# Chunk-selected attention and a gated MLP on one core: K transposed in fp32 with its chunk bounds read from PSUM, odd heads' q and k moved by DMA, loads paced by need, weights held back until the first exps

## The chip, the cores and the metric

The kernel runs on one core of one Trainium2 chip. The metric is device time in microseconds (us) of one execution. Each kernel was executed several times; an execution is called fast or slow by its time against the fastest of the same kernel, and only fast ones are compared. The profiled span is about 2 us shorter than the device time of the same execution (296.9 for 298.89 us before).

Engine names are those of the profile: PE (TensorE matmul), PEld (TensorE weight load), DVE (VectorE), ACT (ScalarE), POOL (GpSimd), SP (SyncE, which here only issues DMAs; "SPq" is its queue). "PEclk" is the clock that TensorE was granted, as a share of full speed.

## The reference, cut to what matters

```python
# q, k, v: (4 batches, 8 heads, 768 positions, 64), fp32
k_chunks = k.reshape(B, H, 24, 32, D)
k_min, k_max = k_chunks.min(axis=3), k_chunks.max(axis=3)
ub = sum_d max(q * k_min, q * k_max)            # an upper bound per query and chunk
top_chunks = the 6 best causal chunks of every query
scores = q @ k.T / 8, masked to the chosen chunks and to the causal part
attn = softmax(scores);  x = attn @ v           # heads side by side: (4, 768, 512)
# then per batch a gated MLP:
h = gelu(x @ w_in); u, v = halves of h; v = layernorm(v) * g_ln
out = x + (u * (w_sg @ v + b_sg)) @ w_out
```

The kernel handles heads in pairs (16 pairs) and selects chunks for groups of four heads (8 groups). A batch is two groups, so there are four MLPs.

## The kernel before: the parts that the change touches

The kernel records operations with their reads, writes, engine and estimated cost. A greedy list planner in the kernel then fixes, before anything runs, the order of instructions on each engine.

Loads, weights and K's side, with cuts marked `...`:

```python
P.base = 60.0
P.op("pool", ...dma_start(winb[:], ...), 8.0, writes=["winb"], dma="winb")      # 3 weight loads,
P.op("pool", ...dma_start(woutb[:], ...), 6.0, writes=["woutb"], dma="woutb")   # ready from the
P.op("pool", ...dma_start(wsgf, ...), 8.0, writes=["wsgf"], dma="wsgf")         # first moment
P.op("sp", ...dma_start(bsgbc[:], ...), 3.0, writes=["bsgbc"], dma="bsg")
...
def loads(p):                       # one pair: k, q, v of two heads, 192 KB each
    s = p % NQS                     # NQS = 3 buffers
    for nm, src, dst in (("kn", k, kn), ("qn", q, qn), ("vn", v, vn)):
        for i in range(2):
            P.op("sp", ...dma_start(dst[s][:, :, i, :], [[DH,128],[128*DH,NT],[1,DH]]), ...)

def kside(p):
    for m, op in ((0, ALU.min), (1, ALU.max)):          # on natural K: transpose + reduce in one op
        P.op("dve", ...tensor_reduce(km[w]..., knv..., axis=AX.X, op=op, apply_transpose=True), ...)
    P.op("dve", ...tensor_tensor(km[w][:, 1], km[w][:, 1], km[w][:, 0], op=ALU.subtract), ...)
    for c in range(4):                                  # bounds to DRAM scratch ...
        P.op("sp", ...dma_start(kscr..., km[w][32*c:32*c+32]...), ...)
    P.op("sp", ...dma_start(W[w][:], kscr...), ...)     # ... and back, transposed
    P.op("pool", ...tensor_copy(kb16[p % 2], knv), ...) # K to bf16
    ...six bf16 PE transposes into one PSUM tile...
    DVE copies rows 0:64 to KA (even head), ACT copies rows 64:128 to KB (odd head)
```

`W` feeds the bound matmuls ("select"). Their result goes through a DVE transpose (`U`), the six-best search (`m8`), a compare (`Dn`), a transpose back (`Dt`) and four mask DMAs into the spare rows of QA and QB. Only then can a head's scores and its exp follow.

The softmax here doesn't subtract the row's maximum and nothing guards it: scores larger than these inputs give would overflow.

## Time and profile before

| | before |
|---|---|
| device time, median (range) of the first three runs | 297.48 us (296.65 to 299.37) |
| first exp starts | 57.8 us |
| PE, DVE, ACT, POOL busy | 73%, 70%, 51%, 35% |
| DMA moved | 30.62 MB in 104,171 packets |

These are lines of the page's second part for the kernel before: the span in 40 equal slices of 7.4 us, busy share in tenths, and the DMA's rate per slice.

```profile
PE   0222027449698739947999999899989999859983
PEclk9999999758999978995999999999999999989999
DMA  8999989669765874434355630031200002200022
GB/s 144 225 218 137 202 151 216 131 136 189 143 131 112 162 134 72 99 61 87 78 152 146 170 82 10 7 97 74 109 0 17 1 2 106 108 2 0 0 107 106
```

For the first six slices, some 44 us, PE is busy for two tenths of the time or less, and the DMA for eight tenths or more. I cut the run where ACT changes work: start to first exp; then heads and MLPs alternate, each MLP beginning with the load of ACT's gelu table (1.28 us at 103.86 us). The next lines are the view by stretches of the kernel before (stretch, length, then each engine's busy us and instructions, granted clock, DMA share, GB/s). The first row is the start, the second the heads until the first gelu, the third the first gelu phase.

```profile
core 0: us, PE busy (x) PEld busy (x) DVE busy (x) ACT busy (x) POOL busy (x), PEclk, DMA share, GB/s
0.00:57.80 57.80, 13.55 (x94) 8.45 (x95) 27.62 (x70) 9.48 (x16) 30.36 (x42) 0.99 1.02 179
57.80:103.86 46.06, 35.28 (x494) 25.02 (x492) 36.00 (x100) 32.31 (x42) 23.50 (x28) 0.87 0.76 145
103.86:128.89 25.03, 19.98 (x156) 9.69 (x160) 14.64 (x48) 10.25 (x18) 2.47 (x3) 0.86 0.55 100
128.89:169.96 41.07, 34.35 (x390) 23.45 (x388) 35.97 (x85) 24.92 (x31) 18.44 (x21) 0.92 0.48 116
...
```

SyncE's timeline of the start (start us, total us, queue, line, what, count) shows what stands in the queue:

```profile
3.04 7.03 SPq L460 DMA_DIRECT2D vn<-in_v_dram  x2
...
25.66 7.14 SPq L477 DMA_DIRECT2D kscr<-km  x3
32.98 1.84 SPq L481 DMA_DIRECT2D W<-kscr  x1
...
53.76 0.87 SPq L568 DMA_DIRECT2D QA<-Dt  x1
```

Two V loads took 7.03 us to issue, where the pairs before them took 1.03 and 1.13 us. What held them up the trace does not show. Three scratch stores took another 7.14 us. The first mask copy goes out at 53.76 us. The waits of the first 60 us (engine and line, what it waited for: us in total, times, longest) name the same thing from PE's side:

```profile
PE PST L509 <- DMA qn<-in_q_dram: 21.8, 3, 12.2
...
PE PST L539 <- DMA W<-kscr: 16.1, 1, 16.1
```

Groups by line and shape (busy us, mean ns of one | idle before) give the costs on DVE that the change touches: the transposing reduces, the copy of K, the strided `U` transposes, the subtraction.

```profile
L470 DVE TRANSPOSE_TENSOR_REDUCE km<-kn 128x24 f32<-128x768 f32 x32 | 30.1, 958 | 10.9 <-DMA kn<-in_k_dram 10.9
L547 DVE STREAM_TRANSPOSE U<-PST 128x288 f32<-128x288 f32 x16 | 11.0, 687 | 27.6 <-PE PST L539 27.6
L498 DVE COPY KA<-PST 64x768 bf16<-64x768 bf16 x16 | 8.5, 534 | 3.9 <-PE PST L490 3.7
L474 DVE TENSOR_TENSOR km<-km 128x32 f32<-128x32 f32 x16 | 6.3, 392 | 0.1
```

Last, the head of the chain of waits (the work that ended last, followed back; shares of the span):

```profile
PE 39%; DVE 20%; SPq 15%; issue 10%; DMA 9%; ACT 3%; POOL 3%; POOLq 0%; DVEq 0%
```

### The profile page before, as it was taken

How to read it: one execution, taken by the hardware profiler on the slowest of the kernel's cores; microseconds unless marked ns; L12 is line 12 of the kernel's file. 1: busy time of each engine (PE TensorE's matmuls, PEld its weight loads, DVE VectorE, ACT ScalarE, POOL GpSimd, SP SyncE). 2: the span in 40 equal slices, each digit the busy share in tenths (PEclk: the TensorE clock that was granted, in tenths of full speed). 3: DMA queues.
4: the chain of work that ended last, by engine and by line, in shares of the span. 5: the costliest groups of instructions: out<-in, count | busy, mean ns of one | idle time of the engine just before them, and what ended most of it. 6: DMA issues, size and time to landing. Idle time of an engine off the chain costs nothing.

```text
span 296.9 us, 5806 instructions
## 1 busy us (share of the span) xinstructions
PE 216.7 (73%) x2198; PEld 134.2 (45%) x2212; DVE 207.6 (70%) x539; ACT 150.3 (51%) x208; POOL 104.2 (35%) x126
## 2 busy tenths in 40 slices
PE   0222027449698739947999999899989999859983
PEld 0111004326556514534766665676663576634431
DVE  7853008449689946497997797988685787626884
ACT  1111005243779922762555975865877774646300
POOL 8994008152546620142433831354440121201000
PEclk9999999758999978995999999999999999989999
DMA  8999989669765874434355630031200002200022
GB/s 144 225 218 137 202 151 216 131 136 189 143 131 112 162 134 72 99 61 87 78 152 146 170 82 10 7 97 74 109 0 17 1 2 106 108 2 0 0 107 106
DMA packets 104171, 30.62 MB, mean 103 GB/s; under 512 B 98384, under 2 KB 100432, under 8 KB 104144
## 3 DMA queue, kind: packets, MB, share of 16 engines
q1 hardware_dynamic: 102304, 27.51, 43.3%
q0 software_dynamic: 1840, 2.75, 5.6%
q8 instruction: 17, 0.28, 0.4%
q14 instruction: 10, 0.08, 0.1%
HBM read 25.30 MB, written 6.82 MB: 108 GB/s over the span
## 4 chain that ended last, share of the span: by engine, by line
PE 39%; DVE 20%; SPq 15%; issue 10%; DMA 9%; ACT 3%; POOL 3%; POOLq 0%; DVEq 0%
SPq L460 9%; PE PSM L713 9%; PE PSC L596 8%; PE PSM L733 6%; DMA kn<-in_k_dram 5%; PE PST L539 4%; SPq L477 4%; PE PSM L615 4%; DVE vhat L686 3%; DVE km L470 3%; ACT E L601 2%; PE PSM L696 2%; DVE stats L677 2%; DVE U L547 2%; PE PSM L670 2%
## 5 line engine op out<-in xcount | busy, mean ns | idle before, releaser
L601 ACT ACTIVATE E<-PSC 128x1024 bf16<-128x1024 f32 (+1 forms) x96 | 84.7, 918 | 51.9 <-PE PSC L596 50.9
L605 POOL TENSOR_SCALAR_AFFINE_SELECT E<-E 128x768 bf16<-128x768 bf16 x32 | 28.6, 893 | 58.8 <-ACT E L601 58.5
L713 PE MATMUL PSM<-wsgT,vhat 128*128 128x384 bf16 x192 | 37.4, 338 | 5.6 <-DVE vhat L686 5.3
L470 DVE TRANSPOSE_TENSOR_REDUCE km<-kn 128x24 f32<-128x768 f32 x32 | 30.1, 958 | 10.9 <-DMA kn<-in_k_dram 10.9
L509 PE MATMUL PST<-identF,qn 128*128 128x128 f32 x96 | 17.3, 306 | 24.4 <-DMA qn<-in_q_dram 21.8
L596 PE MATMUL PSC<-QA,KA 88*128 88x128 bf16 (+1 forms) x224 | 26.3, 255 | 9.0 <-DMA QA<-Dt 6.8
L547 DVE STREAM_TRANSPOSE U<-PST 128x288 f32<-128x288 f32 x16 | 11.0, 687 | 27.6 <-PE PST L539 27.6
L670 PE MATMUL PSM<-winb,xT 128*128 128x512 bf16 x90 | 23.5, 406 | 8.2 <-DVE km L474 6.0
L596 PE MATMUL PSC<-QB,KB 128*128 128x128 bf16 (+1 forms) x224 | 25.4, 252 | 3.4 <-ACT E L601 3.4
L514 ACT ACTIVATE qT<-PST 128x384 f32<-128x384 f32 x32 | 15.6, 496 | 24.0 <-PE PST L509 23.4
L539 PE MATMUL PST<-qT,W 64*32 64x288 f32 x128 | 13.4, 497 | 19.1 <-DMA W<-kscr 18.6
L713 PEld LDWEIGHTS PSM<-wsgT,vhat 128*128 128x128 bf16 x192 | 17.9, 100 | 18.1 <-DVE vhat L686 5.1
L696 PE MATMUL PSM<-xT,winb 128*128 128x384 bf16 x128 | 24.6, 333 | 0.1
L509 PEld LDWEIGHTS PST<-identF,qn 128*128 128x128 f32 x96 | 12.2, 156 | 27.7 <-DMA qn<-in_q_dram 12.2
L720 DVE SCALAR_TENSOR_TENSOR vsT<-PSM,glnT,bsgbc 128x384 f32<-128x384 f32 x32 | 19.6, 612 | 6.7 <-PE PSM L713 6.5
L733 PE MATMUL PSM<-woutb,uT 128*128 128x512 bf16 x88 | 21.6, 379 | 3.5 <-DVE uT L724 3.2
L596 PEld LDWEIGHTS PSC<-QA,KA 88*128 88x128 bf16 x224 | 16.4, 101 | 16.2 <-DMA QA<-Dt 4.6
L499 ACT ACTIVATE KB<-PST 64x768 bf16<-64x768 bf16 x16 | 12.9, 806 | 20.9 <-PE PST L490 20.6
L674 ACT ACTIVATE vgb<-PSM 128x512 f32<-128x512 f32 x24 | 14.2, 596 | 18.2 <-PE PSM L670 18.1
L677 DVE BATCH_NORM_STATS2 stats<-vgb 128x6 f32<-128x512 f32 x24 | 16.1, 680 | 8.0 <-ACT vgb L674 7.9
L701 ACT ACTIVATE uT<-PSM 128x384 bf16<-128x384 f32 x32 | 15.7, 491 | 11.5 <-PE PSM L696 11.1
L615 PE MATMUL PSM<-vx,E 128*128 128x65 bf16 x480 | 20.1, 194 | 1.6 <-ACT E L601 1.4
(66 smaller groups left out, 371.3 us busy)
## 6 DMA issues: line engine op xcount, KB each, us to landing
kn<-in_k_dram SPq DMA_DIRECT2D x32, 192.0 KB, 3.5
qn<-in_q_dram SPq DMA_DIRECT2D x32, 192.0 KB, 3.7
vn<-in_v_dram SPq DMA_DIRECT2D x32, 192.0 KB, 3.6
out_dram<-osb SPq DMA_DIRECT2D x24, 256.0 KB, 2.0
vgb<-in_moe_w_sg_dram POOLq DMA_DIRECT2D x1, 1152.0 KB, 13.5
winb<-in_moe_w_in_dram POOLq DMA_DIRECT2D x1, 1024.0 KB, 9.5
kscr<-km SPq DMA_DIRECT2D x64, 8.0 KB, 2.1
woutb<-in_moe_w_out_dram POOLq DMA_DIRECT2D x1, 512.0 KB, 7.4
```

What stands on the lines that cost most here:

```text
L460: P.op("sp", lambda e, i=i, src=src, dst=dst: e.dma_start(dst[s][:, :, i, :], bass.AP(src.tensor, (2 * p + i) * S * DH, [[DH, 128], [128 * ...
L470: P.op("dve", lambda d, m=m, op=op: d.tensor_reduce(km[w][:, m, :, 0:NT].rearrange("p h j -> p j h"), knv.rearrange("p (a x) -> p a x", x= ...
L509: r = e.matmul(t.ap()[:, 128 * j:128 * j + 128], qn[s][:, 3 * hf + j].rearrange("p i d -> p (i d)"), identF[:], is_transpose=True)
L539: r = e.matmul(t.ap()[32 * j:32 * j + 32, 0:n], W[w][lo:lo + 64, m, :], rhs, start=(m == 0), stop=(m == 1), tile_position=(lo, 32 * j))
L596: r = e.matmul(t.ap()[:, o:o + n], kt_[rows, 128 * kb:128 * kb + 128], qt_[rows, q0:q0 + n], start=True, stop=True, skip_group_check=True)
L601: P.op("act", lambda e, t=t, c0=c0, c1=c1: e.activation(E[es][:, c0:c1], t.ap()[:, 0:c1 - c0], ACTF.Exp, scale=SCALE), act(c1 - c0), reads ...
L605: P.op("pool", lambda g: g.affine_select(ev, ev, pattern=[[0, NT], [1, 128]], compare_op=ALU.is_ge, fill=0.0, base=0, channel_multiplier=- ...
L615: r = e.matmul(t.ap()[:, 65 * qb:65 * qb + 65], E[es][:, a:a + 128], vx[w][:, kb, i, :], start=first, stop=False, skip_group_check=True)
L670: r = e.matmul(t.ap()[:, 0:F], xT[s][:, dk, 128 * qt:128 * qt + 128], winb[:, dk, F:DFF], start=(dk == 0), stop=(dk == NDK - 1))
L696: r = e.matmul(t.ap()[:, 0:TG], winb[:, dk, 128 * fb:128 * fb + 128], xT[s][:, dk, TG * tg:TG * tg + TG], start=(dk == 0), stop=(dk == NDK ...
L713: r = e.matmul(t.ap()[:, 0:TG], vhat[s][:, sb, 128 * fb:128 * fb + 128], wsgT[:, sb, TG * tg:TG * tg + TG], start=(sb == 0), stop=(sb == N ...
L733: r = e.matmul(t.ap()[:, 0:DM], gT[s][:, fb, 128 * qt:128 * qt + 128], woutb[:, fb, :], start=(fb == 0), stop=(fb == NF - 1))
```

## The change

Its intent is to reach the first exp sooner and to relieve DVE and POOL. K is transposed in fp32 by PE, so chunk minima and maxima are plain reductions of the PSUM tile, already in the layout that the bound matmuls need. That removes the scratch trip, K's cast on POOL and DVE's K copy. One full-height ACT copy (or POOL cast, for q) serves both heads, and a DMA inside SBUF moves the odd head's half. Loads come as all k, all q, all v of a group, at most four in flight, and the weights wait for the first heads. The full diff also does smaller things that the cut leaves out: it brings the weights in 14 pieces for 3, builds K's indicator mask once for eight times, moves the w_sg transposes behind the sixth head, and gives the planner another model of DMA times. Cut to its core:

```diff
+WINDOW = 4
...
+                    if o.bulk and len(flight) >= WINDOW:
+                        t = max(t, ops[flight[-WINDOW]].end)
...
+            if o.bulk:
+                if len(flight) >= WINDOW:
+                    o.deps[flight[-WINDOW]] = True        # a load waits for the fourth before it
+                flight.append(i)
...
+            for x in reversed(t.ops):                     # readers of one PSUM tile on different
+                if x.eng != eng:                          # engines go one after the other
+                    deps.setdefault(x.idx, False)
...
+        def weights(h):
+            after = [("E", h % 3, 0)]                     # two weight pieces after each of heads 0..6
...
-            for m, op in ((0, ALU.min), (1, ALU.max)):
-                P.op("dve", ...tensor_reduce(km[w]..., apply_transpose=True), ...)
-            ...four scratch stores, one scratch load, POOL cast, bf16 transposes, copies to KA and KB...
+            for hf in range(2):
+                ...three fp32 transposes of kn into one PSUM tile t...
+                for m, op in ((0, ALU.min), (1, ALU.max)):
+                    P.op("dve", ...tensor_reduce(W[w][:, m, 12*hf:12*hf+12], t..., axis=AX.X, op=op), ...)
+                P.op("act", ...activation(KA[w][:, TG*hf:TG*hf+TG], t.ap()[:, 0:TG], ACTF.Copy), ...)
+            P.op("sp", ...dma_start(KB[w][64:128, :], KA[w][64:128, :]), ...)
+            P.op("sp", ...dma_start(KA[w][64:64 + NC, :], IND[0:NC, :]), ...)   # indicator rows again
...
-            P.op("pool", ...tensor_copy(QA[w][0:64, :], qT[w][0:64, :]), ...)
-            P.op("pool", ...tensor_copy(QB[w][64:128, :], qT[w][64:128, :]), ...)
+            P.op("pool", ...tensor_copy(QA[w][:], qT[w][:]), ...)
+            P.op("sp", ...dma_start(QB[w][64:128, :], QA[w][64:128, :]), ...)
...
-                    U[u][:, ...].rearrange("p b (j c) -> p b c j", c=4),
-                    t.ap()[:, 0:n].rearrange("p (b c j) -> p b c j", c=4, j=8)),
+                    U[u][:].rearrange("p b c -> p (b c)")[:, n * hf:n * hf + n], t.ap()[:, 0:n]),
...
-                for p in (2 * g, 2 * g + 1):
-                    loads(p); kside(p); qside(p)
+                for p in pr: loads(p, (("kn", k, kn),))
+                for p in pr: loads(p, (("qn", q, qn),)); kside(p)
+                for p in pr: qside(p)
+                for p in pr: loads(p, (("vn", v, vn),)); vside(p)
```

## The prediction

> **What bounds the kernel now.** Two regimes. The page's slices show the first 60 us with the DMA at 0.7 to 0.9 and PE at 0.0 to 0.4; ScalarE's timeline has the first exp at 57.8 us. By stretches, over 20 to 42 us PE is busy 1.5 us and the DMA share is 0.99 at 163 GB/s. SyncE issues 18 loads of 192 KB for three pairs in a row, [...]and the key bounds' scratch stores queue behind them, so that the bound matmuls wait 16.1 us for W. Some 11 MB move before the first exp; four heads need 2.4 MB. In the chain of waits SyncE's queue is 15% and DMA 9%, most of it before 60 us. [...]a fully busy DMA moves 160 to 200 GB/s.
> From 150 to 250 us PE is busy 24 of every 25 us: PE-bound. Between (58 to 150 us) PE has 70 of 92 us, with the first gelu phase stretched (25 us against 12 for the third).
>
> **Costs.** Removed: 80 scratch issues of tiny packets; transposing reduces on DVE, 30.1 us; their subtractions, 6.3 to about 2; DVE's KA copies, 8.5; POOL's casts of K, 13.2; half of the Q casts, 14; most of the initial memsets and masks. Added: 64 reduces of 384 fp32 from PSUM, estimated 0.55 us each from XS (0.549) and vsT (0.612): 35 us of DVE; ACT copies of K 16 us for 12.9; fp32 transposes on PE: six take 0.83 us against 0.50 for bf16, about +5 us in all; 48 small SBUF copies[...]. DVE loses some 15 us, POOL about 30, PE gains 5, ACT 3.
>
> **On the path.** Start: four k loads, then four q loads (1.6 MB plus the bias at about 180 GB/s, estimated 11 to 13 us with landing); last q transposes and copies 2; bounds, transposes, max, compare, transpose 8; mask DMA and scores 4. First exp at 26 us (22 to 32): -32 us.
> Heads 0 to 7 take 46 us now (57.8 to 103.9); I expect 38 to 42, as group 2 and 3 preparation falls in it. The first gelu phase should shrink from 25 to 16 to 20 us. Against this, preparation hidden in the idle first 58 us moves into PE-bound time, and the +5 us of PE lies there too: +5 to +9. Later phases keep their length; the tail after the last exp (35 us) is untouched.
> Sum: 297.5 - 32 - 5 - 7 + 6, about **259 us**, range **246 to 273**. Chances: faster by over 2% 0.97, within 2% 0.02, slower 0.01.
>
> **What would show it.** First exp near 26 us; SyncE's queue below 5% of the chain; no wait on W; six fp32 K transposes in 0.83 us; reduces near 0.55 us; first gelu table load near 66 us instead of 103.9; PE above 80% of the span; DMA no longer saturated from 25 us on; last gelu load to end still about 35 us.
>
> **What would make it wrong.** SyncE issues in order, so a load held back by pacing, or a key copy waiting on ACT, blocks a mask DMA behind it: first exp 35 us or later. Each K tile holds one of two PSUM buffers through matmul, two reduces and a copy in series (about 2.3 us): bounds, Q and xT transposes could queue there, and PE wait. Late weights would hold the first gelu phase. [...]

297.5 - 32 - 5 - 7 + 6 is 259.5. The 160 to 200 GB/s of a busy DMA are read from the kernel before: 163 GB/s at a DMA share of 0.99 from 20 to 42 us, 179 at 1.02 over the start. The times under "On the path" are my estimates.

## The result, and the profile after

The changed kernel takes 265.42 us median (265.08 to 270.07, 4 runs; the 270.07 is a slow run: it counts in the median, not in the ratio), against 297.79 us before (4 runs). The ratio is 0.8906, with a 95% interval of 0.8853 to 0.8959. A ratio here is the mean time of one kernel's fast runs over that of the other's fast runs of the same rounds, so it is not quite the ratio of the medians.

The lines of the page after (slices of 6.6 us) that answer to those before:

```profile
PE   1674797685989996999989999998998999779884
PEclk9996779798699999899999999999999999999999
DMA  7996999999998799436757331223110030200033
```

The empty start of PE is gone. But the DMA stays nearly full for twelve slices, the fifth to the sixteenth, and PEclk still dips several times (I come back to these dips under e12). By stretches, with the cuts at the same events:

```profile
core 0: us, PE busy (x) PEld busy (x) DVE busy (x) ACT busy (x) POOL busy (x), PEclk, DMA share, GB/s
0.00:27.25 27.25, 14.41 (x78) 8.49 (x79) 15.89 (x58) 6.84 (x13) 6.78 (x17) 0.91 0.92 167
27.25:84.89 57.64, 46.73 (x557) 33.04 (x557) 34.13 (x125) 36.31 (x53) 26.57 (x36) 0.86 1.13 212
84.89:99.04 14.15, 13.64 (x99) 8.77 (x101) 11.00 (x27) 12.38 (x25) 3.40 (x4) 1.00 1.04 199
99.04:136.21 37.17, 34.16 (x406) 24.23 (x402) 31.80 (x82) 22.95 (x30) 12.17 (x14) 0.95 0.65 160
...
```

Put side by side, in us of the two profiled spans:

| stretch | before | after | difference |
|---|---|---|---|
| start to first exp | 57.8 | 27.2 | -30.6 |
| heads until the first gelu | 46.1 | 57.6 | +11.6 |
| first gelu phase | 25.0 | 14.2 | -10.9 |
| all after it | 168.0 | 164.5 | -3.5 |
| span | 296.9 | 263.5 | -33.4 |

So nearly the whole gain, 30.6 of 33.4 us, is the start. After the first exp, before took 239.1 us and after takes 236.3. The two middle rows belong together (71.1 against 71.8 us): the heads became longer and the gelu phase behind them shorter. It is no extra idling: in the heads phase PE was not busy for 10.8 us before (46.06 less 35.28) and for 10.9 us after (57.64 less 46.73). The phase is longer by PE's busy time. The groups of PE's lines within that phase say by which: transposes of q 33 for 18 (6.9 us for 2.7), 31 fp32 transposes of k for 30 bf16 ones (5.8 for 2.8), 96 bound matmuls for 64 (10.0 for 7.4). That is 9.8 of the 11.4 us. Preparation of later groups, which the kernel before had done in its idle start or did in its gelu phase, now lies between the first heads.

SyncE's timeline now has the four k loads, then four q loads, and its first mask copy at 22.95 us instead of 53.76:

```profile
0.79 2.20 SPq L489 DMA_DIRECT2D kn<-in_k_dram  x4
3.03 0.58 SPq L476 DMA_DIRECT2D bsgbc<-in_moe_b_sg_dram  x1
...
4.13 4.37 SPq L489 DMA_DIRECT2D qn<-in_q_dram  x4
...
22.95 0.79 SPq L588 DMA_DIRECT2D QA<-Dt  x1
```

The groups by shape after, for the new reduces, the plain `U` transposes, the subtraction and ACT's copy of K:

```profile
L507 DVE TENSOR_REDUCE W<-PST 128x12 f32<-128x384 f32 x64 | 32.8, 543 | 6.6 <-PE PST L501 6.4
L568 DVE STREAM_TRANSPOSE U<-PST 128x288 f32<-128x288 f32 x16 | 7.6, 475 | 11.3 <-PE PST L560 11.3
L514 DVE TENSOR_TENSOR W<-W 128x24 f32<-128x24 f32 x16 | 3.3, 209 | 0.2
L510 ACT ACTIVATE KA<-PST 128x384 bf16<-128x384 f32 x32 | 15.8, 494 | 22.7 <-DVE W L507 22.6
```

The reduces cost 543 ns each (0.55 us was the estimate). `U` fell from 687 to 475 ns with chunks in natural order and a contiguous write (e2, which brings the permuted write back, has 690 ns), a gain of 3.4 us of DVE that I had overlooked. The last line shows ACT idle until DVE had done both reduces, 22.6 us in all, which is the price of the planner's rule that readers take turns at a PSUM tile. The chain of waits after:

```profile
PE 46%; DVE 17%; DMA 10%; ACT 9%; issue 7%; SPq 5%; POOL 4%; POOLq 1%
```

### The profile page after: what moved, and what is told of

Its sections match the earlier page's. It is cut to its first block, busy times and chain, and to the rows that moved or that the text cites. A ratio compares the mean times of both kernels' runs of the same rounds, so it can differ in the third digit from the quotient of the medians.

```text
span 263.5 us, 5701 instructions
## 1 busy us (share of the span) xinstructions
PE 222.7 (85%) x2198; PEld 142.5 (54%) x2212; DVE 192.7 (73%) x546; ACT 149.9 (57%) x224; POOL 71.6 (27%) x95
## 3 DMA queue, kind: packets, MB, share of 16 engines
q0 software_dynamic: 2016, 2.75, 6.4%
## 4 chain that ended last, share of the span: by engine, by line
PE 46%; DVE 17%; DMA 10%; ACT 9%; issue 7%; SPq 5%; POOL 4%; POOLq 1%
PE PSM L733 9%; PE PSC L616 9%; PE PSM L753 7%; ACT E L621 6%; DMA qn<-in_q_dram 5%; DVE vhat L706 5%; PE PST L560 4%; PE PSM L690 4%; DMA vn<-in_v_dram 4%; PE PSM L635 4%; SPq L489 3%; PE PST L528 2%; DVE vsT L740 2%; PE PST L501 2%; DVE uT L744 2%
## 5 line engine op out<-in xcount | busy, mean ns | idle before, releaser
L733 PE MATMUL PSM<-wsgT,vhat 128*128 128x384 bf16 x192 | 35.4, 328 | 4.1 <-DVE vhat L706 2.5
L507 DVE TENSOR_REDUCE W<-PST 128x12 f32<-128x384 f32 x64 | 32.8, 543 | 6.6 <-PE PST L501 6.4
L616 PE MATMUL PSC<-QA,KA 88*128 88x128 bf16 (+2 forms) x224 | 27.6, 262 | 3.1 <-DMA QA<-Dt 2.2
L510 ACT ACTIVATE KA<-PST 128x384 bf16<-128x384 f32 x32 | 15.8, 494 | 22.7 <-DVE W L507 22.6
L616 PE MATMUL PSC<-QB,KB 128*128 128x128 bf16 (+2 forms) x224 | 26.3, 252 | 1.8 <-ACT E L621 1.8
L501 PE MATMUL PST<-identF,kn 128*128 128x128 f32 x96 | 18.0, 309 | 10.7 <-POOL IND L451 4.6
L616 PEld LDWEIGHTS PSC<-QA,KA 88*128 88x128 bf16 x224 | 17.8, 104 | 11.3 <-DMA QA<-Dt 2.7
L635 PEld LDWEIGHTS PSM<-vx,E 128*128 128x128 bf16 x480 | 18.3, 100 | 10.1 <-POOL E L625 4.2
L539 POOL CAST QA<-qT 128x768 bf16<-128x768 f32 x16 | 14.4, 899 | 29.1 <-ACT qT L533 26.8
L545 POOL CAST vx<-vn 128x768 bf16<-128x768 f32 x16 | 13.5, 843 | 32.4 <-PE PSM L642 22.3
L744 DVE TENSOR_TENSOR uT<-vsT,uT 128x384 bf16<-128x384 f32 x32 | 20.0, 629 | 0.6
L759 DVE TENSOR_TENSOR osb<-PSM,XS 128x512 f32<-128x512 f32 x24 | 16.5, 688 | 5.4 <-PE PSM L753 5.2
```

What stands on the lines that cost most here:

```text
L507: P.op("dve", lambda d, t=t, m=m, op=op, hf=hf: d.tensor_reduce(W[w][:, m, 12 * hf:12 * hf + 12], t.ap()[:, 0:TG].rearrange("p (c x) -> p ...
L616: r = e.matmul(t.ap()[:, o:o + n], kt_[rows, 128 * kb:128 * kb + 128], qt_[rows, q0:q0 + n], start=True, stop=True, skip_group_check=True)
L635: r = e.matmul(t.ap()[:, 65 * qb:65 * qb + 65], E[es][:, a:a + 128], vx[w][:, kb, i, :], start=first, stop=False, skip_group_check=True)
L733: r = e.matmul(t.ap()[:, 0:TG], vhat[s][:, sb, 128 * fb:128 * fb + 128], wsgT[:, sb, TG * tg:TG * tg + TG], start=(sb == 0), stop=(sb == N ...
L744: P.op("dve", lambda d, fb=fb, tg=tg, vs=vs: d.tensor_tensor(gT[s][:, fb, TG * tg:TG * tg + TG], vsT[vs][:], uT[s][:, fb, TG * tg:TG * tg ...
```

## The experiments

Theories at the outset. **A**: the start is a DMA queue, and what counts is which bytes go ahead of the first exp. Rival **B**: the scratch trip of the bounds alone held the start. For the heads phase, which had become 11.6 us longer: **C**, it is bound by DMA bytes (share 1.13). Rival **D**: it is bound by something else, POOL's order or PE. For the last round, **E**: after the first exp the kernel is bound by PE and its order. Rival **F**: by DMA or DVE.

Each label below states the difference to the changed kernel. In e1 to e8 the planner made a new order for the edited program, so such a run shows the edit and a new order together. In e9 to e12 the orders of PE, DVE, ACT and POOL were compared with those of the changed kernel before running, and they are the same (in e9 but for the matmuls left out); SyncE's is the same but for the load sizes in e11 and the moved bias in e12. (The traces show the same order of PE's lines in e9 to e12 as in the changed kernel, and clearly other orders in e1 and e3 to e7.) Stretches are quoted as start / heads / first gelu / rest, in us, of the one profiled execution. Medians are over all runs of a kernel, slow ones too (one in after, e2, e8, e9, e11 and e12, two in e10).

| run | ratio to before (95%) | median us | start / heads / gelu / rest |
|---|---|---|---|
| before | 1 | 297.8 | 57.8 / 46.1 / 25.0 / 168.0 |
| after | 0.8906 (0.8853 to 0.8959) | 265.4 | 27.2 / 57.6 / 14.2 / 164.5 |
| e1 loads as before | 0.9227 (0.9172 to 0.9283) | 275.3 | 38.2 / 42.8 / 16.7 / 175.8 |
| e2 K as before | 0.9401 (0.9337 to 0.9466) | 280.7 | profile fell in a slow run |
| e3 weights early | 0.9460 (0.9395 to 0.9525) | 281.0 | 41.0 / 44.9 / 16.4 / 177.3 |
| e4 no pacing | 0.8950 (0.8892 to 0.9008) | 267.1 | 30.4 / 56.6 / 15.7 / 162.8 |
| e5 half of the loads | 0.9134 (0.9059 to 0.9209) | 272.7 | 27.3 / 61.5 / 15.3 / 166.6 |
| e6 copies by engines | 0.9355 (0.9265 to 0.9444) | 279.4 | 28.2 / 57.1 / 14.3 / 175.6 |
| e7 V cast on DVE | 0.9064 (0.8970 to 0.9157) | 269.8 | 27.9 / 57.6 / 15.5 / 167.0 |
| e8 later loads gated | 0.9558 (0.9459 to 0.9657) | 285.8 | 27.4 / 59.5 / 15.1 / 181.2 |
| e9 less PE | 0.8782 (0.8741 to 0.8824) | 262.7 | 25.6 / 60.2 / 14.1 / 161.6 |
| e10 less DVE | 0.8921 (0.8872 to 0.8970) | 267.2 | 27.1 / 59.7 / 14.2 / 162.5 |
| e11 less DMA | 0.8785 (0.8740 to 0.8829) | 262.5 | 27.5 / 54.3 / 14.2 / 164.4 |
| e12 bias later | 0.9013 (0.8978 to 0.9048) | 269.1 | 26.9 / 61.9 / 14.2 / 164.5 |

e5, e9, e10 and e11 give wrong results on purpose. The others are correct.

### e1: the loads as before

```diff
-WINDOW = 4
+WINDOW = 1000
-            after = [("E", h % 3, 0)]
+            after = []
...            (k, q, v of a pair issued together, as before)
```

> The changed kernel with the three load changes undone (k, q, v of a pair in one go, no pacing, weights at the start); K's fp32 transposes, bounds from PSUM and DMA copies stay. Theory A (the start is a DMA queue: what counts is which bytes go first): first exp still late, 38 to 46 us against 27.3, and the total gives back 10 to 18 us, 275 to 283. Rival B (the scratch round trip of the bounds alone held the start): first exp at 30 us or less, total within 4 us of 265.

The first exp came at 38.2 us and the time at 275.3 us, both where theory A had put them. K's new side alone, with the old loads, is thus worth 7.7% (ratio 0.9227), and it moves the first exp from 57.8 to 38.2 us. B, as the sole cause, falls; that the scratch trip has a large share in the start stands.

### e2: K's side as before

```diff
-            ...fp32 transposes, reduces from PSUM, SBUF copy by DMA...
+            ...transposing reduces, kscr stores and load, POOL cast, bf16 transposes (as before)...
```

> The changed kernel with K's side as before (bf16 cast on POOL, transposing reduces, DRAM scratch), loads ordered, paced and weights late as after. Theory A: first exp at 30 to 36 us, total 270 to 278, so the loads alone bring over half of the gain. Rival B: W again waits behind the scratch, first exp above 42 us, total above 284.

280.7 us, between the two bands. The profile fell in a slow run, so of its stretches I use only the first exp, at 34.0 us, which A had put at 30 to 36. The loads alone are worth 6.0% of the 10.9%, so a little over half of the gain, as A had said, though the time missed A's band. Together with e1 this makes a square by ratio: neither 1, loads only 0.9401, K only 0.9227, both 0.8906. The product of the two single ratios is 0.867, so the two parts overlap a little, and neither replaces the other. The square is not clean: its corner "neither" is the kernel before, which also lacks the smaller changes (the planner's DMA model, the mask built once, the full-height q cast), and no run undoes those alone.

### e3: weights early

```diff
-            after = [("E", h % 3, 0)]
+            after = []
```

> Only the wait of the weights for the first exps is undone. 2.75 MB more go ahead of the first exp: at about 200 GB/s up to 14 us if they share evenly, so first exp 32 to 40 us. If heads 0 to 7 are bound by DMA (theory C), those bytes are then missing from that phase, it gets shorter by about as much, and the total is 264 to 270. If heads 0 to 7 are bound by something else (rival D), the delay of the first exp stays, and the total is 272 to 280.

One line costs 15.6 us by the medians, with the new order that it brings. The first exp moved by 13.8 us, to 41.0, close to what 2.75 MB take at 200 GB/s (13.75 us; the changed kernel's DMA moved 212 GB/s over the heads). The heads phase did get 12.7 us shorter, as C had expected, but the total did not profit: the rest got 12.8 us longer (177.3 against 164.5). PE ran 461 instructions in the heads phase for 557 in the changed kernel, and the preparation that was missing there came later. SyncE's timeline shows how the delay adds up:

```profile
4.37 5.66 SPq L489 DMA_DIRECT2D qn<-in_q_dram  x3
12.28 6.84 SPq L516 DMA_DIRECT2D KB<-KA  x1
19.16 0.58 SPq L489 DMA_DIRECT2D qn<-in_q_dram  x1
```

In this order a copy of K stands ahead of the fourth q load. It could not go before K was there, and its issue took 6.84 us, so the last q load of the first group left at 19.16 us. In the changed kernel all four had left by 8.5 us.

### e4: no pacing

```diff
-WINDOW = 4
+WINDOW = 1000
```

> Only the window of four loads in flight is removed; the order of k, q, v stays. Theory A: [...]first exp 30 to 38 us; with C the phase of heads 0 to 7 gets shorter by as much, total 264 to 271. If pacing is what counts: total above 273.

First exp 3.2 us later, total 267.1 us, both in A's bands, and the interval of the ratio overlaps that of the changed kernel. Of the load changes, the pacing is the one whose own worth these runs do not show.

**What A comes to.** For each run the bytes ahead of the first exp can be worked out as the start's GB/s times its length (before: 179 times 57.8 is 10.3 MB; after: 167 times 27.25 is 4.6 MB):

| run | MB moved before the first exp | first exp, us | PE idle before it, us | span against after, us |
|---|---|---|---|---|
| before | 10.3 | 57.8 | 44.3 | +33.4 |
| e3 weights early | 7.1 | 41.0 | 28.4 | +16.1 |
| e1 loads as before | 7.2 | 38.2 | 23.8 | +10.0 |
| e4 no pacing | 5.7 | 30.4 | 12.3 | +2.0 |
| after | 4.6 | 27.2 | 12.8 | 0 |
| e12 bias later | 4.2 | 26.9 | 12.0 | +4.0 |

From after to before it is 30.6 us for 5.8 MB, 190 GB/s, which is the rate of a busy DMA here (179 GB/s over the start before, 212 over the heads after). By itself this line proves nothing: a DMA that is always busy moves bytes in proportion to the length of the start, whatever holds the first exp. What carries A is that e3 put 2.75 MB ahead and nothing else, and e1 only undid the loads (each with a new order), and the first exp came 13.8 and 11.0 us later. The last two columns show how this reaches the total: what PE idles more in the start than in the changed kernel (31.4, 15.6 and 10.9 us) is close to what the span loses. The stretches behind trade preparation among each other: e1, too, has shorter heads, by 14.8 us, and a longer rest, by 11.3. At 4.6 MB and below, the bytes no longer decide; see e12.

### e5: half of the loads

```diff
-                for i in range(2):
+                for i in range(2 if p < NQS else 1):      # odd head: stale data from the fourth pair on
```

> Wrong result on purpose: from the fourth pair on, the odd head's q, k and v are not loaded and the buffer's old data is used; every engine does the same instructions. It takes some 4 MB, about 20 us of DMA at 200 GB/s, out of the time up to the first gelu. Theory C (heads 0 to 7 are bound by DMA): first exp unchanged near 27 us, exps to first gelu table load 38 to 44 us instead of 57.6, total 248 to 254. Rival D (POOL's queue in order, or PE and its PSUM buffers): 54 us or more, total within 4 us of 265.

This run went against C: the DMA's share over the heads fell to 0.79, and the phase became longer, 61.5 us, with a total of 272.7 us outside both bands. But the planner had made another order, so the run could not tell an unimportant DMA from a worse order. That is why e11 repeats it with the order kept.

### e6: the odd head's copies by engines

```diff
-                P.op("act", ...activation(KA[w][:, ...], t.ap()[:, 0:TG], ACTF.Copy), ...)
+                for kt_, lo in ((KA[w], 0), (KB[w], 64)):
+                    P.op("act", ...activation(kt_[lo:lo + 64, ...], t.ap()[lo:lo + 64, 0:TG], ...)...)
-            P.op("pool", ...tensor_copy(QA[w][:], qT[w][:]), ...)   and the SBUF DMAs
+            ...two half-height POOL copies...
```

> The odd head's q and k are written by POOL and ACT again (two half-height copies instead of one and a DMA); no SBUF copies by DMA but the mask rows. Some 3.6 MB less DMA in the whole run, about 2 MB or 10 us of it before the first gelu, against 16 us more ACT and 14 us more POOL in the whole run. Theory C: heads 0 to 7 shorter by 5 to 10 us, total 257 to 263. Rival D: no shorter, and ACT's extra work makes the total 266 to 272.

279.4 us, worse than both bands. The heads phase did not get shorter (57.1). The loss lies in the rest, 175.6 against 164.5 us. A half-height ACT copy takes as long as a full one (0.48 us against 0.49), so the second one doubles the 15.8 us, and the PSUM tile is held that much longer; POOL works 15.4 us more. Moving half of a copy by DMA may thus be a large part of what the change brings (0.9355 against 0.8906), and I had priced it as a small relief of POOL. The order is new here too, and no run separates it, ACT's copies and POOL's casts.

### e7: V's cast on DVE

```diff
-            P.op("pool", lambda g: g.tensor_copy(vx[w][:, :, :, 0:DH], vn[s][:]), ...)
+            P.op("dve", lambda g: g.tensor_copy(vx[w][:, :, :, 0:DH], vn[s][:]), ...)
```

> V's cast moves from POOL to DVE, so that a late V no longer holds back POOL's masks of the heads. If POOL's order is what stretches heads 0 to 7 (rival D): that phase 46 to 50 us, total 255 to 260. Theory C: the wait reappears elsewhere, phase 54 to 60 us, total 262 to 268.

In the changed kernel POOL waited 9.6 us for V in the heads phase, with the heads' masks behind it in its order. Taking V's cast away left the phase at 57.6 us, to the tenth, and the total, 269.8 us, came out above both bands. This speaks against POOL's wait for V as what stretches the phase; as the order is new and DVE has the cast, it does not settle it.

### e8: later loads gated

```diff
+            after = [("E", (4 * (g_ - 2) + j) % 3, 0)] if g_ >= 2 else []
...
+                        reads=after, writes=[(nm, s, i)], dma=..., bulk=True)
```

> The loads of group g (from 2 on) wait for masks of heads of group g-2 (k for its second head, q third, v fourth), so heads 0 to 7 do not share the DMA with groups 3 and 4. Theory C: heads 0 to 7 take 46 to 52 us, the moved bytes fall in later phases where the DMA has room, total 257 to 263. Rival D: phase unchanged, total 264 to 268; if the gate is too tight, later groups come late and the total is above 268.

285.8 us. The heads phase stayed (59.5) and the rest grew to 181.2 us: as I read it, the gate was too tight, and later groups came late. With the new order in it, the gate's own price is not separated. It was meant as an improvement on a theory that e11 then largely removed.

### e9: less PE work in the same order

```diff
-                    for m in range(2):
+                    for m in range(1):            # the bound without its second half
```

> Wrong result on purpose: the second half of the bound matmuls (rT with the differences) is left out; the order of instructions on every engine is the same. PE loses 128 matmuls, some 9 us at full clock (16 of them take 1.15 us), 2 us of it before the first exp. Theory E (after the first exp the kernel is bound by PE and what it waits for in its order): total 255 to 258. Rival F (bound by DMA bytes or by DVE): only the 2 us of the start, 262 to 264.

The total, 262.7 us, lies in F's band, but its stretches do not speak for F. The start lost 1.6 us, as planned. The first row of the next view is the heads, the second the next eight heads with the first MLP's second part:

```profile
25.64:85.81 60.17, 44.43 (x511) 32.70 (x509) 34.94 (x125) 36.31 (x54) 26.76 (x36) 0.86 1.13 202
...
100.00:135.50 35.50, 31.86 (x393) 22.71 (x390) 31.76 (x82) 22.91 (x30) 12.16 (x14) 1.00 0.73 174
```

From the end of the first gelu phase to the last gelu table load, the changed kernel takes 130.7 us and this one 126.2. There 64 matmuls are missing, 16 in each of four stretches. In the changed kernel's timeline eight of them start 0.49 us before the next eight (55.92 and 56.41 us), so I estimate 0.97 us for 16. Three of these stretches (136.2 to 200.8 us in the changed kernel) are 0.97, 0.95 and 0.97 us shorter: PE's time, paid back one to one. The first, the next heads above, is 1.6 us shorter for another reason. Its missing matmuls only made PE wait longer for `vhat`, 3.01 us for 2.04. But the changed kernel had 3.4 us at half clock in it (PEclk 0.95 for the stretch) and e9 had none; e10, which keeps all matmuls, has none there either and is shorter by the same 1.6 us. The tail behind the last gelu load, which has no such matmul, is 1.6 us longer (35.4 against 33.8), and there it is e9 that has 3.4 us at half clock. The heads phase, with 48 matmuls fewer, took 2.5 us longer. So E holds from 136 to 201 us, and not for the heads.

### e10: less DVE work in the same order

```diff
-                        W[...], t.ap()[:, 0:TG].rearrange("p (c x) -> p c x", x=32),
+                        W[...], t.ap()[:, 0:TG].rearrange("p (c x) -> p c x", x=32)[:, :, 0:8],
```

> Wrong result on purpose: each min and max reads 8 of a chunk's 32 columns, so the 64 reduces shrink from 0.54 us to about 0.25, some 18 us of DVE in all; same order on every engine. K's PSUM tiles are free about 0.6 us sooner each. Theory E: total 262 to 265. Rival F, DVE: 250 to 258.

267.2 us, interval overlapping that of the changed kernel, though its shorter reduces took DVE's busy time from 192.7 to 175.4 us. The row of the next heads:

```profile
101.04:136.59 35.55, 32.94 (x409) 23.03 (x402) 29.67 (x82) 22.95 (x31) 11.88 (x14) 1.00 0.66 162
```

So the reduces on DVE do not bound the total, and neither does the time that they hold a K tile's PSUM buffer. The heads got 2.1 us longer and the rest 2.0 us shorter; 1.6 us of the latter is the half-clock stretch named under e9, which is no effect of the edit that I can see.

### e11: fewer DMA bytes in the same order

```diff
-                        dst[s][:, :, i, :], ... [[DH, 128], [128 * DH, NT], [1, DH]]
+                        dst[s][:, 0:(1 if i and p > 2 else NT), i, :], ... [128 * DH, 1 if i and p > 2 else NT] ...
```

> Wrong result on purpose: as e5, but the odd head's loads from the fourth pair on bring one of six blocks (32 KB for 192 KB) instead of none, so the order on every engine stays as after. 39 loads lose 160 KB each, 6.2 MB of 33.6. Theory E: first exp near 27 us, total 261 to 266. Rival F, DMA: the time to the first gelu falls by over 10 us, total 255 or less. If E holds, e5's loss was its other order.

The rows of heads, first gelu and next heads:

```profile
27.51:81.85 54.34, 44.95 (x558) 31.87 (x557) 35.23 (x125) 36.04 (x53) 26.99 (x36) 0.88 0.90 176
81.85:96.00 14.15, 13.70 (x100) 8.78 (x101) 11.01 (x27) 12.38 (x25) 3.39 (x4) 1.00 0.51 119
96.00:133.20 37.20, 34.52 (x409) 24.28 (x402) 31.76 (x82) 22.99 (x31) 12.18 (x14) 0.95 0.42 114
```

The stretches after the heads are those of the changed kernel to within 0.1 us, with at most two thirds of the DMA share: DMA sets nothing there. In the heads, 22% fewer bytes (9.6 for 12.2 MB, rate times length) are worth 3.3 us, where a phase bound by bytes would have got some 12 us shorter. The traces show where. SyncE's timeline has the first mask copy of the second group; the first line is of the changed kernel:

```profile
42.37 2.70 SPq L588 DMA_DIRECT2D QA<-Dt  x1
```

and the second of e11:

```profile
41.94 0.80 SPq L588 DMA_DIRECT2D QA<-Dt  x1
```

PE's timeline of the changed kernel shows what the late copy did (in brackets: idle time before, and what ended it):

```profile
46.97 0.52 PE L528 MATMUL PST<-identF,qn 128*128 128x128 f32 x3
49.46 0.86 PE L616 MATMUL PSC<-QA,KA 88*128 88x384 bf16 x4 [1.97 <-DMA QA<-Dt]
50.11 0.84 PE L528 MATMUL PST<-identF,qn 128*128 128x128 f32 x3
```

PE paused 1.97 us for the mask, and the same three transposes that took 0.52 us before the pause took 0.84 us after it: PEclk was 0.53 over 49.6 to 53.2 us. In e11 this pause is not there and the clock stays at 1.00. The pause and about half of the 3.4 us at half clock are worth some 3.6 us, which is about what e11 gained. So, as far as these two traces show, the bytes cost time by one late mask copy, not by the rate of the loads. C, which asked for over 10 us, falls. And e5 against e11 (spans of 270.6 and 260.4 us) had nearly the same loads left out: those 10 us are, for the most part, the planner's other order.

### e12: bias later

```diff
         P.schedule()
+        ...on SyncE, move the bias and gain loads behind the first four mask copies...
```

> Correct result: only the bias (384 KB) and gain loads move on SyncE from between k and q to behind the first four mask copies; the other engines keep their order. If the bytes ahead of the first exp still set it: 2 us less at 190 GB/s, first exp near 25 us, total 262.5 to 264. If the first exp hangs on the chain of transposes, bounds, max and mask alone: first exp within 0.5 us of 27.3, total within 1 us of 265.4.

The start gained only 0.3 us, so with 4.6 MB or less ahead of the first exp the chain of transposes, bounds, search and mask sets it, not the bytes. The total got 1.2% worse, which neither theory had, all of it in the heads phase; compare the first gelu and the next heads with the rows above:

```profile
26.92:88.85 61.93, 47.19 (x558) 34.12 (x557) 34.58 (x125) 36.61 (x53) 27.08 (x36) 0.81 1.08 203
88.85:103.00 14.15, 13.70 (x100) 8.77 (x101) 11.01 (x27) 12.38 (x25) 3.39 (x4) 1.00 1.03 194
103.00:140.20 37.20, 34.52 (x409) 24.21 (x402) 31.80 (x82) 22.98 (x31) 12.18 (x14) 0.95 0.66 164
```

The granted clock of that phase was 0.81 instead of 0.86, and PE's timeline of e12 shows three pauses that the changed kernel lacks or has shorter:

```profile
32.18 1.51 PE L528 MATMUL PST<-identF,qn 128*128 128x128 f32 x6 [3.05 <-DMA qn<-in_q_dram]
...
51.23 0.88 PE L528 MATMUL PST<-identF,qn 128*128 128x128 f32 x3 [2.48 <-issue]
54.52 1.03 PE L616 MATMUL PSC<-QA,KA 88*128 88x384 bf16 x4 [2.42 <-DMA QA<-Dt]
```

The moved bias now went out just ahead of two q loads of the second group, and PE waited 3.05 us for one of them. Read in steps of 0.4 us, PEclk is at one half for stretches of about 3.4 us or a multiple of it (13.7, 6.8, 6.8 and 3.4 us in the kernel before), and at 1.00 otherwise. In the heads phase of e12 those stretches add up to about 23 us, in the changed kernel to 16, in e11 to 12.5, in the kernel before to 12. They mostly follow pauses: of five in the changed kernel four begin in or just behind a pause of 1.7 to 3.4 us, those at 22.2 us (pause 3.37 us, then 6.8 us at half clock), 49.6 (1.97, then 3.4), 63.2 (1.72, then 6.8) and 104.2 us (2.04, then 3.4); the fifth, 3.4 us at 32.6 us, follows only a pause of 0.64 us. Not every pause has one: before 80.59 us the kernel before paused 2.43 us and kept its clock. The wait for `vhat` before the next heads, of 2.04 or 2.05 us, was followed by a fall in the changed kernel, e11 and e12 and by none in e10, nor in e9, where it lasted 3.01 us. So the length of a pause does not tell here whether a fall follows, and what else decides it is not shown. Where one follows, the time lost is the pause and slower matmuls behind it (0.84 for 0.52 us in the timeline under e11). That the pause causes the fall is read from the traces and not shown by a run of its own, since no run set the clock. For reading the table it means that one such stretch more or less can come between two executions without any edit: the fast executions of the changed kernel have mean clocks of 0.955, 0.961 and 0.968 over spans of 263.5, 263.3 and 263.9 us, which comes to 23.7, 20.5 and 16.9 us at one half if all the loss is at one half. I estimate at most 1.7 us for a stretch of 3.4 us; these three spans do not show it.

The clock record also says too little of the start. It stands at 1.00 until 22 us, yet eight bound matmuls took 1.18 us at 16.33 us, and the same eight took 0.66 us at 55.92 us, also with 1.00 on record; at 33.37 us, with half clock on record, they took 1.20 us. PE's timeline of the changed kernel, at the start and in the heads phase:

```profile
16.33 1.18 PE L560 MATMUL PST<-rT,W 64*32 64x288 f32 x8
...
55.92 0.66 PE L560 MATMUL PST<-rT,W 64*32 64x288 f32 x8
```

No correct version beat the changed kernel. The three that take work away in its order (e9 to e11) show what a version could aim at, not how.

## Why the prediction was right, and where its steps failed

The time, 265.4 us, lies within the stated range of 246 to 273 and 6.4 us above the estimate of 259. Point by point:

- **"First exp at 26 us (22 to 32): -32 us."** Right: 27.2 us, -30.6. The mechanism, bytes and scratch ahead of the first group, was tested by e1 to e4 (with new orders). The first mask copy went out at 22.95 us. The estimate of 1.6 MB ahead was too simple; 4.6 MB moved, since V and the next group's loads run alongside, and at that point it is the chain of work that counts (e12).
- **The costs.** Right: reduces 543 ns for 0.55 us estimated, ACT's K copies 15.8 us for 16, DVE as a whole 207.6 to 192.7 us for "some 15 us", POOL 104.2 to 71.6 for "about 30", PE 216.7 to 222.7 for "gains 5". ACT stayed at 150 us, where 3 more were expected. DVE's total fits partly by luck: the 3.4 us of `U` (687 to 475 ns each, permuted write against plain) were not in the sum. The SBUF copies took 3.9 and 4.2 us to land (KB from KA, QB from QA). SyncE's queue in the chain fell to 5%, the edge of what I wrote.
- **"Heads 0 to 7 ... I expect 38 to 42", and the first gelu table load "near 66 us".** Wrong: 57.6 us and 84.9 us. The step that failed first is where the moved preparation goes: the prediction lets preparation of groups 2 and 3 fall into the heads and yet shortens them, and books what leaves the idle start, with PE's 5 us more, to later phases. What filled the heads is PE work: 46.7 us busy for 35.3 us before, at a clock of 0.86 (0.87 before). "DMA no longer saturated from 25 us on" failed too: the DMA stayed nearly full, at 212 GB/s in the heads, until 100 us. But that weighed little: where e11 took the bytes away, the phase gave only 3.3 us.
- **"The first gelu phase should shrink from 25 to 16 to 20 us."** In size better than said, 14.2 us, but it is the other side of the same shift: heads and gelu phase together went from 71.1 to 71.8 us. The term that I entered as -12 for both was +0.7. The preparation that before did in its idle start, and in a long gelu phase, now lies in the heads.
- **"+5 to +9" for preparation and slower PE in later phases.** Wrong in sign: all after the first gelu phase is 3.5 us shorter. I entered the moved preparation there, and it went into the heads instead. So the two mis-sized terms partly cancelled: +12.7 us and -9.5 us, and +1.4 us from the start, against the profiled spans.
- **The warnings.** "SyncE issues in order, so ... blocks a mask DMA behind it" did not happen at the start, but in a small way at 42 us, where the mask was ready at 40.3 us, its first copy stood behind three q loads, issued from 38.89 us on, until 42.37 us and then took 2.70 us to issue (e11 shows its price). Queueing at the PSUM buffers as a limit is made unlikely by e10, which shortened the two reduces and gained nothing. (A K tile's work adds up to 2.1 us in the changed kernel at full clock: 0.50 for its three transposes, two reduces of 0.543, 0.494 for the copy.) Late weights did not hold the first gelu phase (14.2 us). The warning on the granted clock named a cause that no trace shows: by the timelines under e11 and e12, most falls follow a pause of PE, though not every pause brings one. Over the whole span PEclk was at one half for some 31 us before and some 24 us after, so the recorded clock did not turn against the change (of the first 22 us the record says too little, see under e12).

What stays open: the order of the work in the heads phase, and what the smaller changes of the diff are worth by themselves. Its length, 57.6 us, is 46.7 us of PE busy time, of which the stretches at half clock account, by my estimate, for at most about 8 us (half of 16), and 10.9 us of pauses, 2 of them for one mask copy. Whether an order with the same preparation would have fewer pauses there was not tried; e9 and e10 took work out of the phase without making it shorter (60.2 and 59.7 us), e9 even with longer pauses (one of 4.20 us for POOL's work on an `E` tile).

## What to carry to other kernels

Ask what the first unit of real work needs, and let nothing else go ahead of it on the DMA: here one line that makes the weights wait is worth about 15 us, as much as a redesign of K's side (both measured with the planner's new order), while the pacing of loads by itself showed nothing. What a late start cost here was about the time that PE idled in it; the length of the next stretch alone says little, since preparation moves between stretches. A share of 100% on the DMA is not a bound until a run with fewer bytes and the same order says so (e11: 22% fewer bytes, 3.3 us of some 12). Where a planner chooses the order, compare runs of one order only, since a new order alone moved the time here by some 10 us (e5 against e11).
